# Attention and gated FFN on one core: other orders of work for its 32 rounds, and two moved steps

## The chip, the cores and the metric

The kernel runs on one core of one Trainium2 chip. The metric is device microseconds of that core for one execution; lower is better. The core's engines are named as the profile names them: PE (TensorE, with PEld for its weight loads), DVE (VectorE), ACT (ScalarE), POOL (GpSimd) and SP (SyncE, which here only issues DMAs). Each engine works through its own queue in order, and engines wait for each other by semaphores.

## What is computed

Input x has 2048 rows of 448. Two branches are mixed row by row with a gate g:

```python
qkv = (x @ wqkv).reshape(B, S, 3, H, Dh)                 # H = 16 heads, Dh = 28
p = softmax(einsum("bhqd,bhkd->bhqk", q, k) * Dh ** -0.5)
a = einsum("bhqk,bhkd->bhqd", p, v) @ wo
gate = x @ W_gate; gate = gate * (gate > 0)              # F = 1792
b = (gate * (x @ W_up)) @ W_down
g = sigmoid((x * gate_w).sum(-1))
out = g * a + (1 - g) * b
```

All inputs and the output are float32. For accuracy, most operands are split into a high part and the rest ("low"), and a product is a sum of several matmuls: 11 of them (TERMS) for a product over 448, three for the down projection.

## The kernel before

**Stages.** A prologue (up to about 96 us) casts x and the projection weights, computes queries and keys of the first heads and all values, and begins with head 0. Then come 32 **rounds**, two for each head: round v handles half of the keys (8 tiles of 128) of head v // 2 for all 2048 queries. A tail finishes the gate-and-up products, does the down projection and the output projection `wo`, mixes and stores.

**Orders written out by hand.** What is issued in a round stands in a string (R0 to R31, lines 49 to 91; the list ROUNDS, line 93, says which round uses which). The loop from line 787 reads the letters one by one. Each letter issues one step, and since every engine's queue is in order, the string sets the order on all of them:

- x: one of the 11 matmuls of a unit of the query-and-key projection (`qk_mm`) or of gate and up (`gu_mm`), 128x128 by 512 columns. After the eleventh, the result leaves PSUM: a gate unit by ACT (`relu`), an up unit by DVE (`hidden`), then DMAs.
- s: `score`, two matmuls for 2 x 512 scores. Part of the scores (raw) are copied to SBUF by ACT, and DVE also reads them from PSUM, in b; the others (direct), whose row maximum is already in the query's extra rows, go through ACT's exp at once.
- m: `smax`, two matmuls of scores of a later head of which only the maximum is kept (DVE). n: `smax_end`, which transposes those maxima and sends them by DMA into that head's queries.
- b: `block_min`, running minimum of negated raw scores (DVE). A: `all_max`, which makes of it the maximum for each query (DVE, several small steps). g: `take_max`, subtraction of that maximum from a tile of 2048 (POOL). e and E: `take_exp`, exp of half or all of such a tile (ACT).
- P and Q: `pv`, the two halves of the product of exps and values, with PE as four independent column groups of 32. c and f: `rescale`. N: `normalise`, on POOL, of the head before, which needs a DMA of reciprocal row sums. w: casts of gate-and-up weights. D: casts of down weights.

**PSUM.** s and m take turns over three buffers of two banks each (`ps_w`, line 137), so each of them can only start once the one three before has been read out. x units, P and n share two further banks (`ps_x`).

**Around the two moved steps.** In the prologue, `qk(tb, c)` is one unit: block tb of 512 rows, output rows c. Unit 0 of all four blocks holds keys and queries of head 0; its results go to DRAM by POOL's DMA queue, in turns through one of two forms (line 463), and `load_k(0)` and `load_q(0)` (lines 542, 543) read them back on SP's and POOL's queues. In the tail a list `todo` (lines 968 to 980) is run in order. `down(i)` is 12 matmuls with h tile i; `gate_up(i)` is 22 matmuls, followed by the load of weights for tile i + 2 into the freed one of two buffers, and by the write of h. Four of the 56 gate-and-up tiles, 52 to 55, are left for the tail (`done` = 52): 52 and 53 ahead of the first `down`, 54 and 55 between later ones.

Of the kernel before, what the change touches and what calls it, by code (L numbers as in the profile page):

```python
# [48 lines left out]
R0 = "xxbbsssxxxxsxbxmxxxsxxxxxssxxxxsxAxsxxxxxxmxxxxxgsbsxexxebxxsxxxgmxbxxmePAeQ"

R1 = "nsmsxxsgbxbxsxxxgxsxxbxsxxxsxsxxxssAxxmxxsxmsxxmxxxmxgmgExexxxxsxmsxsxxexbsxxbEcxxebmxPeNAfQ"

R2 = "smsxggbxxsxsxxxsxxbxsbxxxxxssxxxsxxAxggsmxxsxsxExxxmmsxxxmxxxsxsxexbxxxxbxsmebxeeAexPemmQ"

R3 = "gsmNsxsbxsxwxsbbExxxAxxssmxxwxgxxsxxxxxxxwxmEmcsnxxxgxgxxsxxxsxmxsxxxxmmxfExsxxmxxxssbbsbeePAQw"

R4 = "smsxxsbxxxwwxxsxxbsgbxxxsxxmsxsxxsxsxsAxmxwxsxxsmsgxgxxxExxbxmxxeexmmxxgxsPbxEesxembwQAx"

R5 = "NsxxsxxssbgxxxbxxxxwbxxxxsmnxsxsmAsxxswgsxsxxEmxxmxxxxsxxsxmxxEmxxmgsbxexxxxsxxmbegxscbefPeAwwQ"

R6 = "smsxxxxgxbwssgxxxxxxxsxxxbbxxwemxAssxxxssxsxxmxxsxxsmsxgxexmmsexgbexxxxxsEbemPsewmxwQbxAx"

R7 = "wssxxbxxsNbxxsbxxxxxgwxsxxxsxmsxsxxxxAsxsgxsxxmnxmxxxesxwsgexmmxxsxbsxxxxcexxsbbAexxmPEgmexfemQw"

R8 = "smsxgxxswsxxxbxsxwbxbxxsxAxsxxssxgxsmxxgsxxsxmgxxExmxsEmxxmxxwxsxmsbPExxexbmxsxbAxexwQx"

R9 = "ssxsxbxsxxbxbxxxNxxsxsxAxgxggssxxxxsxsxmmExxsxxmxxsxxmwxmxsxxwmxwexsxnesEbbcsPxgmbxeAxxxxfxemQw"

R10 = "sxswxxsgxxxxxbsxwxsxgbwbxsxxAxxesxgxxxxssxxmsxxsxxmsxexmxsxEmxxmxxsxgxbwmEmPEmsxbsxxQbA"
# [12 lines left out]

R17 = "smsxxbxsxxsxbNxbxxsxgxsxxxssxxAxxnxssmxxexxxmxsmxgxxmesxxsxmgxxEmExgmsxxcxxbxsexbsfbePAQ"

R18 = "xgsmsxbxsxxxbxxsbxxsxxAsxxxsgsxxssxxxxmsxexmxxxsxxgsmxxemxexxmxesmgEePsebmxxsbbxAQ"

R29 = "sxxsxxssxxxbxxxxgxxEbgxxsxxbxxsxsxsxxNxxxxsAxxsxssnxsxxxcxsxxxxxxggExxExxsbxxxxexbxxsbeAfPQxx"

R30 = "DsxxsxgxsxxxxxsxbxsbxxExxxbxxxxssxAxxxxgxsgxsxxsxxxsssxxxxxxxsxEsxxgxExxbexxxxxsebDxxxPbQxA"

R31 = "xxsxxsbxxxxxxsxxbxssxbxxxxxsxxsxxxsxsxxsxxxAxxgxEgxxxxexxxxxgxgsexxNDxexxexxxexDexcsfxPQ"
# [20 lines left out]
def gated_mix_kernel(ctx, tc, x, wq, wo, wgu, wd, out):  # L112
# [40 lines left out]
    def low(dst, src, high):  # L153
        nc.vector.tensor_tensor(dst, src, f32(high), op=OP.subtract)  # L154
# [148 lines left out]
    def all_max():  # L303
        v, j, quads = todo_all.pop(0)
        to = ((0, 11) if j == 2 else (9, 10))[v % 2]
        a, b = (1 - v % 2, 9) if j == 2 else (1, 9 + v % 2)
        nc.vector.tensor_reduce(MN[:, 1:3], R2.pop((v, j)).rearrange("p a (b r) -> p a b r", r=32), axis=AX.X, op=OP.min,  # L307
                                apply_transpose=True)
# [68 lines left out]
    with tc.tile_pool(name="qkv", bufs=1) as pa:
        W = pa.tile([P, 7, VO + VC], F32R, name="W")

        def load_w(c):  # L380
# [82 lines left out]
        def qk(tb, c, terms=TERMS, among=()):  # L463
            ps = ps_any(f"qk_{tb}_{c}")
            for n, (a, b) in enumerate(terms):
                nc.tensor.matmul(ps, W[:, a, c * P:(c + 1) * P], xf(tb, b), start=(n == 0), stop=(n == NT - 1))
# [9 lines left out]
            nc.gpsimd.dma_start(qk_d[c * P:(c + 1) * P, :, tb * TB:(tb + 1) * TB], f32(st))
# [558 lines left out]
```

## Time and profile before

| | |
|---|---|
| median of 3 runs | 1195.46 us (1195.09 to 1198.18) |
| the profiled execution, its own time | 1196.28 us |
| its span from first to last instruction | 1194.5 us |
| PE / PEld busy | 1183.0 / 821.9 us |
| DVE / ACT / POOL busy | 896.9 / 879.0 / 743.3 us |
| mean granted PE clock | 0.999 |

A matmul's shown duration is longer than the distance between two matmuls in a stream, because they are pipelined. So a short wait between two matmuls is not seen as idle time of PE. It is seen in the spacing of their starts, in the length of a stretch that holds a known number of matmuls, and in what PEld, the weight load in front of a matmul, waited for.

In the rows of waits, the numbers are the total in us, how many times, and the longest. In rows of a stretch (A:B), they are its length, then the busy time of PE, PEld, DVE, ACT and POOL with the count of instructions, then the granted PE clock, the share of DMA and GB/s. In rows of the timeline they are the start and the duration in us, the engine, the line, the operation and what it writes and reads; in brackets the idle time before it and what ended it. In rows of groups they are busy us and the mean in ns, then the idle time before them.

### The profile page before, as it was taken

Reading aid. Unit: us, or ns where it says so; the run is one execution under the profiler, and the core shown is the slowest. Engines: PE = TensorE matmul, PEld = TensorE weight load, DVE = VectorE, ACT = ScalarE, POOL = GpSimd, SP = SyncE. Lnnn points to the kernel's source line nnn. Section 1 sums busy time; section 2 is a strip of 40 time slices with the busy share of each in tenths; the row PEclk is TensorE's granted clock in tenths of the full one; section 3 lists DMA queues with packets and bytes.
Section 4 is the critical chain, followed back from the end, with each engine's and each line's share of the span. In section 5 each row is a group of like instructions: output and inputs, shape, how many; then the busy total and the mean of one; then the engine's idle time right before and its main releaser. Section 6 shows DMA issues by size and latency. Waiting matters only on the chain. (4 is left out here: it accounts for less than half of the span.)

```text
span 1194.5 us, 16947 instructions
## 1 busy us (share of the span) xinstructions
PE 1183.0 (99%) x6183; PEld 821.9 (69%) x6183; DVE 896.9 (75%) x1173; ACT 879.0 (74%) x1018; POOL 743.3 (62%) x325
## 2 busy tenths in 40 slices
PE   9999999999999999999999999999999999999998
PEld 6886666666666666666666566666666666899997
DVE  5577888898988888998888898989888553443342
ACT  5237889899999888888888888888888984322121
POOL 5323677898989786777776676767686773421020
PEclk9999999999999999999999999999999999999999
DMA  9994564636373644343445525153534336643342
GB/s 307 283 398 142 193 215 153 179 123 209 120 203 113 211 145 147 116 127 83 142 130 192 144 95 159 41 159 106 155 130 162 121 122 207 210 144 110 116 135 79
DMA packets 70667, 188.86 MB, mean 158 GB/s; under 512 B 13958, under 2 KB 20558, under 8 KB 65678
## 3 DMA queue, kind: packets, MB, share of 16 engines
q1 hardware_dynamic: 65624, 167.31, 45.0%
q0 software_dynamic: 4480, 19.99, 4.4%
q8 instruction: 49, 0.80, 0.3%
q10 hardware_dynamic: 480, 0.47, 0.1%
q14 instruction: 34, 0.28, 0.1%
HBM read 126.96 MB, written 60.96 MB: 157 GB/s over the span
## 5 line engine op out<-in xcount | busy, mean ns | idle before, releaser
L321 POOL TENSOR_TENSOR P<-P,rm 128x2048 f32<-128x2048 f32 x102 | 470.5, 4633 | 118.6 <-DVE rm L315 85.1
L645 PE MATMUL gu<-X,wg 128*128 128x512 f32 x1232 | 365.8, 398 | 2.1 <-DMA wg<-ws_d 2.1
L240 DVE TENSOR_REDUCE mx<-sm 128x1 f32<-128x1024 f32 x256 | 304.3, 1216 | 57.0 <-PE sm L236 55.1
L342 PE MATMUL s<-Q,K 128*128 128x512 f32 x1024 | 319.6, 402 | 2.6 <-DVE mx L240 0.9
L645 PEld LDWEIGHTS gu<-X,wg 128*128 128x128 f32 x1232 | 231.7, 189 | 73.5 <-issue 13.4
L342 PEld LDWEIGHTS s<-Q,K 128*128 128x128 f32 x1024 | 181.9, 188 | 82.5 <-DVE r L292 15.8
L348 ACT ACTIVATE P<-s 128x1024 f32<-128x1024 f32 x204 | 202.0, 1028 | 39.6 <-PE s L342 37.7
L704 PE MATMUL po<-P,V 128*32 128x512 f32 x1640 | 229.9, 595 | 0.0
L346 ACT ACTIVATE P<-s 128x1024 f32<-128x1024 f32 x206 | 201.8, 1032 | 15.8 <-PE s L342 14.0
L332 ACT ACTIVATE P<-P 128x1024 f32<-128x1024 f32 (+1 forms) x154 | 202.1, 1344 | 1.4 <-POOL P L321 1.1
L292 DVE SCALAR_TENSOR_TENSOR r<-s,r 128x1024 f32<-128x1024 f32 x124 | 151.8, 1224 | 20.8 <-ACT P L348 10.2
L236 PE MATMUL sm<-K,Q 128*128 128x512 f32 x520 | 160.7, 398 | 1.4 <-DMA Q<-qk_d 1.4
L704 PEld LDWEIGHTS po<-P,V 128*32 128x32 f32 x1640 | 60.9, 109 | 110.6 <-issue 107.5
L704 PE MATMUL po<-V 128*32 128x512 f32 x408 | 136.8, 594 | 0.0
L321 POOL TENSOR_TENSOR V<-V,rm 128x2048 f32<-128x2048 f32 x24 | 111.2, 4633 | 23.3 <-ACT P L348 18.0
L236 PEld LDWEIGHTS sm<-K,Q 128*128 128x128 f32 x520 | 93.3, 188 | 33.8 <-ACT P L346 4.5
L148 ACT ACTIVATE hh<-hr 128x512 fp32r<-128x512 f32 x52 | 32.8, 632 | 109.2 <-PE acc L939 109.2
L154 DVE TENSOR_TENSOR hh<-hr,hh 128x512 fp32r<-128x512 f32 x52 | 46.6, 900 | 74.1 <-ACT hh L148 73.8
L939 PE MATMUL acc<-WD,hh 128*128 128x448 f32 x480 | 99.3, 365 | 0.0
L939 PEld LDWEIGHTS acc<-WD,hh 128*128 128x128 f32 x480 | 90.1, 188 | 7.3
L292 DVE SCALAR_TENSOR_TENSOR r<-s,P 128x1024 f32<-128x1024 f32 x50 | 61.1, 1223 | 23.7 <-ACT P L348 23.6
L307 DVE TRANSPOSE_TENSOR_REDUCE mn<-r 128x32 f32<-128x1024 f32 x63 | 77.9, 1237 | 1.2
(93 smaller groups left out, 1134.7 us busy)
## 6 DMA issues: line engine op xcount, KB each, us to landing
wg<-ws_d SPq DMA_DIRECT2D x42, 896.0 KB
K<-qk_d SPq DMA_DIRECT2D x32, 448.0 KB
X<-x_d SPq DMA_DIRECT2D x56, 256.0 KB
h_d<-h SPq DMA_DIRECT2D x56, 256.0 KB
Q<-qk_d SPq DMA_DIRECT2D x62, 224.0 KB
hr<-h_d SPq DMA_DIRECT2D x52, 256.0 KB
ws_d<-wg SPq DMA_DIRECT2D x14, 896.0 KB
x_d<-X POOLq DMA_DIRECT2D x8, 1024.0 KB, 15.0
```

Source lines behind the costliest of these rows:

```text
L236: nc.tensor.matmul(ps[:, c, :], Q[h][:, u * P:(u + 1) * P], K[h % 3][:, k0:k0 + TB], start=True, stop=True)
L240: nc.vector.tensor_reduce(to, ps, axis=AX.XY, op=OP.max)
L292: nc.vector.scalar_tensor_tensor(r, ps, -1.0, before, op0=OP.mult, op1=OP.min)
L307: nc.vector.tensor_reduce(MN[:, 1:3], R2.pop((v, j)).rearrange("p a (b r) -> p a b r", r=32), axis=AX.X, op=OP.min, apply_transpose=True)
L321: nc.gpsimd.tensor_tensor(QUAD[q], QUAD[q], m, op=OP.subtract)
L332: nc.scalar.activation(q, q, AF.Exp, scale=-SCALE)
L342: nc.tensor.matmul(ps[:, c], K[h % 3][:, k * P:(k + 1) * P], Q[h][:, j * TB:(j + 1) * TB], start=True, stop=True)
L346: nc.scalar.activation(dst, ps, AF.Exp, scale=SCALE)
L348: nc.scalar.activation(dst, ps, AF.Copy, scale=-1.0)
L645: nc.tensor.matmul(ps, WS[i][:, s, a], xf(i // NF, b), start=(n == 0), stop=(n == NT - 1))
L704: nc.tensor.matmul(po[32 * j:32 * j + 32], V[:, h // 4 % 2, k, h % 4], AT.pop((v, k, j)), start=(k == k0), stop=(k == k0 + NK // 2 - 1))
L939: nc.tensor.matmul(ACC[i // NF][t][:, :D], HH[i][:, a, t * P:(t + 1) * P], wd_high_low(f, b), start=(f == 0 and n == 0), stop=(f == NF - 1 ...
```

## The change

Three edits. (1) All orders are replaced by others with the same counts of s, m, b, g, A per round and, over all rounds, the same 1320 x; rounds 11 to 28 use two orders in turns, R11 and R12, where before they used eight. (2) In the prologue, unit 0 of block 3 is issued before unit 2 of block 1 instead of after it. (3) In the tail, `gate_up(54)` follows `down(4)` instead of `down(2)`, and `gate_up(55)` follows `down(6)` instead of `down(4)`. The diff, with the orders cut to those that the text speaks of most (R0 to R10 and R29 to R31 are replaced in the same way; R13 to R18 fall away):

```diff
-R11 = "sxsxbsxxbgxxxsxxxxsbxxxgsxxsxxssAxsmgnsxxmsxmNxsmxmEExxxxmmsxxxxbxscxxseexxbgefebxxxmAPQ"
-R12 = "sxgssbxgxxxxsbxxxsbxxxxsxxsxssxxsAxmxxsxxsmEmxxsxmxxgxxExmxsgxbsbxsPbExxeAxemmmQ"
-R13 = "sxxsxgxbssxbexbNxxxgxxxsxxxsxxsxxxAsxxsxmnxcsxxsmexxxgxgsmsexxmxxmsxsbxbxxsexEbxeAPmfmemQ"
-R14 = "xsmsxxsbxxxgsexxxxbbAsxxxxsxxsssxxsxxmxgxxgxxsmxsxemxxmsExmxxxxssmPgEbebmsbAxexQx"
+R11 = "ssbnsxxxxsxbxNxbxxggsxxxxsxxxsxsxxssxxAmxsxxemsxmxexxmsxmxxemmgexsbxxxsbcxxxsbxAxmgeePefeQ"
+R12 = "gsmsxxxxssebxxbbxxxsxxxxmxAexxssxgxsxxsxxsmxxsxxemsmexgxexmxxxmsxmxexsbxsgebsebAPQ"
...
 ROUNDS = [
     R0, R1, R2, R3, R4, R5, R6, R7,
-    R8, R9, R10, R11, R12, R13, R14, R15,
-    R16, R17, R18, R11, R12, R13, R14, R15,
-    R16, R17, R18, R11, R12, R29, R30, R31,
+    R8, R9, R10, R11, R12, R11, R12, R11,
+    R12, R11, R12, R11, R12, R11, R12, R11,
+    R12, R11, R12, R11, R12, R29, R30, R31,
 ]
...
         qk(2, 1)
+        qk(3, 0)
         qk(1, 2)
-        qk(3, 0)
         split_w(*w4)
...
-        if i % 2 == 0 and 0 < i and done + 1 + i // 2 < NB * NF:
-            todo.append((gate_up, done + 1 + i // 2))
+        if i % 2 == 0 and 2 < i and done + i // 2 < NB * NF:
+            todo.append((gate_up, done + i // 2))
```

More of the change, by code (lines that the diff above doesn't have):

```diff
@@ L47 @@
 NP = 10
[L49 to L69, printed above, removed]
@@ L71 @@
-R11 = "sxsxbsxxbgxxxsxxxxsbxxxgsxxsxxssAxsmgnsxxmsxmNxsmxmEExxxxmmsxxxxbxscxxseexxbgefebxxxmAPQ"
-R12 = "sxgssbxgxxxxsbxxxsbxxxxsxxsxssxxsAxmxxsxxsmEmxxsxmxxgxxExmxsgxbsbxsPbExxeAxemmmQ"
-R13 = "sxxsxgxbssxbexbNxxxgxxxsxxxsxxsxxxAsxxsxmnxcsxxsmexxxgxgsmsexxmxxmsxsbxbxxsexEbxeAPmfmemQ"
-R14 = "xsmsxxsbxxxgsexxxxbbAsxxxxsxxsssxxsxxmxgxxgxxsmxsxemxxmsExmxxxxssmPgEbebmsbAxexQx"
-R15 = "sNmsxxsxsxxxbgxbxsbxxnxsxxsxsxsxAxxxsmsExgxmxxmxscxsxexmxxxmgxmxxmxxxEsxxbxsxsbePgefebAQ"
-R16 = "sxmsxgxsxxsxxbexbxsxxgxbmAxxxsxsgsxxxxssxmxxsxxsxemxmxgsExxmxxxssmEebPbsmexQxbAxx"
@@ L83 @@
[L83 to L91, printed above, removed]
+R11 = "ssbnsxxxxsxbxNxbxxggsxxxxsxxxsxsxxssxxAmxsxxemsxmxexxmxsmxxemmgexsbxxxsbcxxxsbxAxmgeePefeQ"
@@ new lines @@
+R12 = "gsmsxxxxssebxxbbxxxsxxxxmxAexxssxgsxxsxxsxxmxxsxxemsmexgxexmxxxmsxmxexsbxsgebsebAPQ"
+R0 = "bsxxsbxxxxbsxxssAxxxxxxsxxsxxxmsxxgsxxxxmxsxxsxbgxxxxxxxxbEsxxemxbxxxmxeAPQ"
+R1 = "nsgmsxxssNxxxxxbgxxEbbsmxxxxxxssxsxxxxAsxmxsxxxsExxxmxgmsxxxmxxxxxExmsxmgxxxxxscbssbebAPefQ"
+R2 = "smsxbxxssxbxxxsgxxxsbxgxxxsmsxAxsxsxsxsmxxxxxsxmxEgxxxmmsxxbxxxsexsexgexxxxxbmexxebAxmePQ"
+R3 = "nsgmsxxsgswxxbxwxxbbeAxxssxxxxxsxsxxsexmxxwxmxsNxxxsxmExmxxmxsgxxxxsxxxgmemsxxxxexsxbcbxsPebAfeQw"
+R4 = "smsxxxssbxxxxswxgbwxxbxsxxgsxsAxxsswxxmxgsxexmsxxxsxxmxexsmgxxsxbxxxxxxExxbsExembxemwPQAm"
@@ new lines @@
+R5 = "gsxsxxsbgsxbxxxxxwwxxxbxsmxxwxwsxssAxxxxsmxsxxxnssmxgxExmxmsxxNxxEmxxxmssgEbePbcmsbfeAxxxxxQ"
+R6 = "wssbsxxxxgbsxbxxgxxxxxwxssxxxmwxsmxxsAxsxxxsxxsmxexsxeemxxxgxmsgxxemxxxmxeesseePsbwxbmQbxAx"
+R7 = "ssxNxbwxgssxxxbbxxxxxAxwxswxsxxxsxxxssxmxxxxwEgxmmxnxsxsxxmsxEmxxgxmsxemxxxmgsxbsexbsecbfeAPQ"
+R8 = "wxsmsbxgxxsxxswxxgxbxsbexxxsxxxssxxxAxgssxxxmxxsxmsxxxmexsxxmemegxwsxbEPmsxxbxemxsexbxAwxQ"
+R9 = "sxwsNxxggswsxxxxxxxxxbsxbbxsxxsxsAxxsxxsxgemmxgxsxsxxxmxemxsxmxnEwxxwxxxmsmbEPemscxxsebfbxxAQ"
@@ L93 @@
+R10 = "wsxxxgssxxgxsbxxxxbxwxxxsbxwxsxxsxxsxsAsgxsxxxxmxxxemsxmxexxxmsxExxmxsmbgxxsPEebemmsbAwQ"
+R29 = "sxxsxsxxxbxgxsxxbsxExsxxxxxxxxxbxssxsxAxxxsxgNxxsxsxxxssxxxxgxsxxxExxxbxgxxbxExsexxcxexfxPbAQn"
+R30 = "sgsxxsbxxsxxxxxbxxgxEbxxxxxsxxxxxsssxxxxxsxxsxAsxxxxexgxxxxsxsExxxsexxxbgxxxxsexbxxsexDDbxPQA"
+R31 = "sxsxxsxxxbxxxxxsbbxxxxxxxgsxxxxsxxssxxxxAsxxsxxgxgxgExxxDxxxxNxxxExxEsexcexxsxxfxxxDxPQ"
 ROUNDS = [
     R0, R1, R2, R3, R4, R5, R6, R7,
-    R8, R9, R10, R11, R12, R13, R14, R15,
-    R16, R17, R18, R11, R12, R13, R14, R15,
```

## The prediction

> **What bounds the kernel now.** I read the page first, then who waits on TensorE (PE) and on its weight loads (PEld), then the stretches of the rounds, and the timeline at the three places that the change touches.
>
> ```profile
> span 1194.5 us, 16947 instructions
> PE 1183.0 (99%) x6183; PEld 821.9 (69%) x6183; DVE 896.9 (75%) x1173; ACT 879.0 (74%) x1018; POOL 743.3 (62%) x325
> ```
> ```profile
> PE gu L645 <- DMA wg<-ws_d: 2.1, 1, 2.1
> PE sm L236 <- DMA Q<-qk_d: 1.4, 1, 1.4
> ...
> PEld s L342 <- DVE r L292: 15.8, 39, 0.8
> ...
> PEld s L342 <- ACT P L346: 5.2, 22, 0.5
> ```
>
> PE is busy 1183.0 of 1194.5 us, so only time that PE loses can be won. Two open waits stand out: 2.1 us for gate-and-up weights, 1.4 us for the first query. The rest hides inside "busy", because a matmul's shown duration (about 0.4 us) is longer than its spacing: the weight loads in front of score matmuls wait for VectorE (DVE) or ScalarE (ACT) to empty a PSUM buffer. How much PE loses by that I take from the stretches of the rounds (first number the length; a round ends where its last PV matmul does):
>
> ```profile
> 96.16:410.61 314.45, 313.18 (x1688) 199.86 (x1686) 270.67 (x355) 280.16 (x325) 246.17 (x105) 1.00 0.54 172
> 410.61:914.04 503.43, 502.98 (x2722) 318.21 (x2719) 443.90 (x585) 436.65 (x456) 360.25 (x109) 1.00 0.43 132
> ...
> 150.93:180.12 29.19, 29.19 (x161) 18.77 (x157) 25.90 (x35) 24.84 (x27) 20.95 (x5) 1.00 0.68 218
> 467.33:522.85 55.52, 55.52 (x307) 35.50 (x303) 50.14 (x65) 48.74 (x52) 39.37 (x13) 1.00 0.45 132
> 410.61:467.33 56.72, 56.57 (x306) 34.99 (x302) 49.50 (x69) 48.40 (x50) 41.51 (x13) 1.00 0.50 152
> 941.50:968.71 27.21, 27.21 (x152) 17.98 (x150) 15.14 (x24) 24.41 (x26) 19.87 (x6) 1.00 0.32 98
> ```
> ```profile
> 1025.60 5.32 PE L645 MATMUL gu<-X,wg 128*128 128x512 f32 x22
> 1030.75 0.57 PE L939 MATMUL acc<-WD,hh 128*128 128x448 f32 x2
> ```
>
> The last window row is round 30, my yardstick: its order holds 54 x and 16 s, so 54 + 2·16 = 86 full matmuls, and P beside Q, in 27.21 us, with no wait of PE listed. One matmul more is (1030.75 − 1025.60)/22 = 0.234 us. Orders R11 and R12 hold 40 + 37 x, 32 s and 16 m: 77 + 64 + 32 = 173 matmuls = 2·86 + 1, so a clean pair is 54.65 us. Rounds 11 to 28 hold nine such pairs, 491.8 us clean, and took 503.43: **11.6 us lost**. Rounds 0 to 10 hold 465 x, 172 s and 84 m, 977 matmuls, clean 11·27.21 + 31·0.234 = 306.6, and took 314.45: **7.9 us lost**.
>
> **The change, part by part.**
>
> *1. P beside Q.* Where full matmuls stand between P and Q, PE leaves and enters the four-column form of PV once more. Round 12 has x and m there:
>
> ```profile
> 460.51 0.60 PE L704 MATMUL po<-P,V 128*32 128x512 f32 x3
> ...
> 460.94 0.60 PE L704 MATMUL po<-P,V 128*32 128x512 f32 x3
> ...
> 461.48 0.96 PE L645 MATMUL gu<-X,wg 128*128 128x512 f32 x3
> 462.28 1.55 PE L236 MATMUL sm<-K,Q 128*128 128x512 f32 x6
> 463.76 3.64 PE L704 MATMUL po<-P,V 128*32 128x512 f32 x32
> ```
>
> Leaving takes 461.48 − 460.94 = 0.54 us where the step inside PV is 0.43. Entering takes 463.76 − (462.28 + 5·0.234) = 0.31 instead of 0.234. Parted costs 0.54 + 0.31 − 0.43 − 0.23 = 0.19 us; starts of single matmuls overlap by some 10 ns, so I take 0.2. In the old orders 18 rounds part P from Q (2, 4, 6 to 10, and 11 of rounds 11 to 28), in the new ones five (5, 6, 8, 9, 10): 13·0.2 = **2.6 us less**, 2.2 of it in rounds 11 to 28.
>
> *2. Waits for PSUM.* Scores and maxima (s, m) share three two-bank buffers in turn, so each waits until the one three before it is emptied. Old R11 shows the price of a short distance:
>
> ```profile
> 419.53 0.63 PE L342 MATMUL s<-Q,K 128*128 128x512 f32 x2
> ...
> 420.17 0.30 PEld L236 LDWEIGHTS sm<-K,Q 128*128 128x128 f32 x2 [0.45 <-ACT P L346]
> ```
> ```profile
> L240 DVE TENSOR_REDUCE mx<-sm 128x1 f32<-128x1024 f32 x256 | 304.3, 1216 | 57.0 <-PE sm L236 55.1
> ```
>
> This m follows s, s, x and s; its buffer is that of the first s, whose last matmul ends 0.17 us (0.4 less a step) after its step, so up to the m there are 5·0.234 − 0.17 = 1.0 us of PE work, about as long as one eviction by ACT and shorter than one by DVE (1.216). I counted this distance for all 729 uses in both sets of orders: under 1.1 us, 8 before and none after; under 1.3 us, 63 before and 26 after; in rounds 11 to 28, 45 before and 18 after. So waits should shrink, but a distance isn't a time, since the emptying engine may have other work first. Bounds: all waits gone (each round as clean as round 30), or each pair as bad as the worst old pair, R11 with R12, at 56.72. I take the rows of old R13 with R14 as nearest: 55.52 − 54.65 − 2·0.2 for two parted PVs leaves 0.47 us of waits per pair, with five distances under 1.3 us; the new pair has two. Rounds 11 to 28 then come to 9·(54.65 + 0.47) = 496.1: **7.3 us less**, 2.2 of them from part 1. In rounds 0 to 10, 7.9 − 7·0.2 = 6.5 us are waits; these orders also carry weight casts, and round 2, a plain one of 92 matmuls, lost 29.19 − 27.21 − 6·0.234 = 0.58, of it 0.2 parted. I take 0.4 a round, 4.4 in all: 2.1, and 0.4 from part 1, **2.5 us less**. The three last rounds hold one x more each, the early ones three fewer: nothing in sum.
>
> Other letters move with the orders. n, the transpose of a head's maxima, is the fourth letter of new R11 (the 38th before), so its two small DMAs enter SP's queue some 8 us of PE work sooner, when all maxima of that head are in. N, a product on POOL that needs a DMA, stands in front of that round's first subtractions, as it did in old R13 and R15, which saw no such wait. I cost both at nothing; a late DMA under N would move the subtractions of that round, rival D's mechanism.
>
> *3. Halves of exps.* The new R11 and R12 take every exp in halves (e), where the old orders of rounds 11 to 28 had 35 whole ones (E):
>
> ```profile
> L332 ACT ACTIVATE P<-P 128x1024 f32<-128x1024 f32 x104 | 108.4, 1066 | 1.4 <-POOL P L321 1.1
> ...
> L332 ACT ACTIVATE P<-P 128x2048 f32<-128x2048 f32 x50 | 95.4, 1920 | 0.0
> ```
>
> 35·(2·1066 − 1920) ns = 7.4 us more ACT work. With it ACT has 436.65 + 7.4 = 444 of 496 us, and DVE its 443.9: both 90%. PE covers it; without that cover it is 7.4 us, or 0.4 a round.
>
> *4. The tail.* After down 2 PE stood still for weights of gate-and-up tile 54:
>
> ```profile
> 1004.33 7.46 PE L939 MATMUL acc<-K,hh 128*128 128x448 f32 x36
> 1004.90 0.37 SPq L630 DMA_DIRECT2D wg<-ws_d  x1
> ...
> 1013.09 0.69 DVE L154 TENSOR_TENSOR hh<-hr,hh 128x512 fp32r<-128x512 f32 x1
> ...
> 1013.94 6.96 PE L645 MATMUL gu<-X,wg 128*128 128x512 f32 x22 [2.15 <-DMA wg<-ws_d]
> 1014.59 0.33 SPq L630 DMA_DIRECT2D wg<-ws_d  x1
> ```
> ```profile
> 1014.00:1016.00 2.00, 2.00 (x5) 1.61 (x6) 0.00 (x0) 0.00 (x0) 0.56 (x1) 0.50 0.62 178
> 1018.00:1020.00 2.00, 2.00 (x10) 1.63 (x9) 0.00 (x0) 0.00 (x0) 0.00 (x0) 1.00 0.97 359
> ```
>
> Now downs 3 and 4, 24 matmuls at 7.46/36 = 0.207, fill 1011.8 to 1016.7, and the weights are there at 1013.9. Down 4 needs its cast, done at 1013.78; it starts at 1014.2. Won: the 2.15 us. Behind the wait the granted clock was 0.50, and the 22 matmuls took 6.96 where the next 22 took 5.32: another 1.6, and 0.1 for the first weight load. **3.9 us less**. Tile 55's weights, issued at 1014.59, take the same 9 us, 1023.6, and are wanted at 1016.7 + 5.15 + 4.9 = 26.8: no new wait. The moved step's own write of h and ACT's relu go with it; ACT no longer stands before that relu, so casts and the loads behind them on SP's queue come sooner.
>
> The Trainium skill's page "TensorE: Matmul & The Clock Gate", section "What's actually happening", says that the clock halves after an idle window of about 3.4 us. By it a gap of 2.15 us is too short to count and the tail would give 2.25 us. The row of 0.50 says otherwise here.
>
> *5. The prologue.* Head 0's queries and keys wait for unit 0 of all four blocks; that of block 3 now runs one unit (11·0.234 = 2.6 us) sooner.
>
> ```profile
> 21.96 2.40 DVE L154 TENSOR_TENSOR X<-xr,X 128x1024 fp32r<-128x1024 f32 x2
> ...
> 32.17 0.67 POOL L476 DMA_DIRECT2D qk_d<-K  x1 [1.35 <-DVE K L154]
> ...
> 35.56 1.03 POOL L211 DMA_DIRECT2D Q<-qk_d  x2 [2.71 <-DMA qk_d<-K]
> 36.24 2.05 SPq L211 DMA_DIRECT2D Q<-qk_d  x2
> ...
> 47.14 0.70 PE L236 MATMUL sm<-K,Q 128*128 128x512 f32 x2 [1.39 <-DMA Q<-qk_d]
> ```
>
> Block 3 is cast by 24.4, and its unit would start near 25.3: nothing to wait for. But sends alternate, so it now leaves in two DMAs by the other buffers, and the other unit's write stands before the query loads on POOL's queue. Of 2.6 us some 1.5 remains at the loads. They land among other transfers, so bounds are 0 and 1.5 (the 1.39 and the first load's delay); I take **1.2 us less**.
>
> *Sum:* 7.3 + 2.5 + 3.9 + 1.2 = 14.9 us off the profiled execution's 1196.28 (its span and 1.8 around it): 1181.4. The runs' median is 0.8 below that execution, so **1180.6 us**.
>
> **Rivals.**
>
> *A, the waits only move.* Three buffers and engines at 90% may shift each wait to the next use. Then parts 1, 4 and 5 remain: 1196.28 − 2.6 − 3.9 − 1.2 − 0.8 = 1187.8. For it: most uses between 1.3 and 2 us keep a similar count, 264 before and 325 after. Against: single waits above 0.1 us stand at the short distances.
>
> *B, all rounds clean.* 11.6 + 7.9 − 5·0.2 + 5.1 = 23.6 less: 1171.9. Round 30 does it, but without maxima.
>
> *C, nothing to measure.* The two new orders are repeated nine times, a bad wait with them: nine pairs like old R11 with R12, less its parting, 56.5 us, are 508.6, 5.2 over before. With 2.5 + 3.9 + 1.2 won elsewhere, 1193. The change would then not do what its words say ("more distance"). Against: 18 short uses instead of 45.
>
> *D, slower: exps too late for Q in odd rounds.* New R11 ends "AxmgeePefeQ": P beside Q, with the last two exps behind P.
>
> ```profile
> 417.33 1.25 DVE L307 TRANSPOSE_TENSOR_REDUCE mn<-r 128x32 f32<-128x1024 f32 x1
> ...
> 419.97 0.71 DVE L315 STREAM_TRANSPOSE rm<-mn 128x512 f32<-128x512 f32 x1
> ```
> ```profile
> L321 POOL TENSOR_TENSOR P<-P,rm 128x2048 f32<-128x2048 f32 x102 | 470.5, 4633 | 118.6 <-DVE rm L315 85.1
> ```
>
> Its second all_max stands 9.6 us into the round's PE work; it takes 420.68 − 417.33 = 3.35, two subtractions 9.27, an exp 1.07: 23.3, where Q starts at 24.0. Late by more than 0.7 us, Q waits. Three DVE evictions more in front, 3.7 us, would cost 3.0 in each of nine odd rounds, 27 us. With parts 1, 4 and 5 and no other wait won: 1187.8 + 27 = 1215. Against: DVE may run that step ahead of its place, as its inputs are complete after the block minima 6 us earlier.
>
> **How the numbers follow.** Chances: forecast (1176 to 1185) 0.48, A 0.23, B 0.13, C 0.10, D 0.06. The range 1171.5 to 1191 leaves out C, D and what of B lies lower. No change means within 0.3%, 3.6 us. Forecast, A and B lie below that, 0.84 and a little of C: faster 0.85, same 0.09, slower 0.06.
>
> **What would show it.** Right: rounds 11 to 28 near 496 us, pairs near 55.1; the weight loads' waits for DVE before scores well under 15.8 us; no wait of PE for weights and no clock of 0.50 past 1000 us; the wait for the first query under 0.4. Wrong: a pair above 55.9, PV matmuls spaced over 0.43 in odd rounds, ACT without idle time, or a new wait of PE in the tail.

## The result and the profile after

| | before | after |
|---|---|---|
| median of 4 runs each | 1195.53 us (1195.09 to 1198.18) | 1184.28 us (1184.05 to 1184.62) |
| the profiled execution, its own time | 1196.28 us | 1184.21 us |
| its span | 1194.5 us | 1182.4 us |

The ratio after to before is 0.9901, with a 95% interval of 0.9884 to 0.9919. The forecast was 1180.6 us with a range of 1171.5 to 1191: the sign and the range hold, and the time is 3.7 us above the forecast.

The first lines of the page of after, the span and the busy time of each engine:

```profile
span 1182.4 us, 17006 instructions
PE 1175.0 (99%) x6183; PEld 821.2 (69%) x6183; DVE 894.1 (76%) x1173; ACT 877.2 (74%) x1054; POOL 743.3 (63%) x325
```

ACT has 36 instructions more (1054 against 1018): the exps that are now taken in halves. PE has the same 6183 matmuls in a span 12.1 us shorter.

Who waits, in the trace of after (total us, times, longest):

```profile
PEld s L330 <- DVE r L280: 10.4, 36, 0.8
PEld s L330 <- DVE mn L289: 9.2, 11, 0.8
PEld s L330 <- ACT P L334: 5.4, 24, 0.7
PEld sm L224 <- ACT P L334: 4.6, 22, 0.4
...
PE s L330 <- DVE mx L228: 0.9, 1, 0.9
PE s L330 <- DVE mn L590: 0.4, 1, 0.4
PE s L330 <- ACT P L334: 0.2, 1, 0.2
```

The line numbers are 12 lower than before, so L330 is the old L342. The two open waits that the prediction named (2.1 us for tile 54's weights, 1.4 us for the first query) are no longer in the list. The weight loads' wait for DVE's r is 10.4 us where it was 15.8. The 9.2 us under DVE's mn (1.7 before) are hardly waits for a buffer: these 11 waits are 0.84 us each and stand at the first score of a round, right behind PV, where before the same 0.84 stood under other names (mx, rm, r). So this list alone doesn't measure what the rounds won; the lengths of the stretches do.

The stretches of after (length, busy PE, PEld, DVE, ACT, POOL with counts, clock, DMA share, GB/s), and then two pairs of the new orders R11 and R12, rounds 13 and 14, and 15 and 16:

```profile
0.00:95.67 95.67, 92.70 (x401) 74.11 (x401) 61.84 (x71) 39.36 (x80) 35.17 (x59) 1.00 0.89 313
95.67:406.81 311.14, 310.72 (x1683) 200.89 (x1684) 269.20 (x353) 279.84 (x327) 245.32 (x104) 1.00 0.54 169
406.81:905.06 498.25, 498.11 (x2723) 317.29 (x2719) 442.02 (x585) 435.05 (x491) 359.68 (x110) 1.00 0.45 136
905.06:985.76 80.70, 80.67 (x451) 53.10 (x447) 41.96 (x65) 71.62 (x76) 64.24 (x23) 1.00 0.38 114
985.76:1182.40 196.64, 192.81 (x940) 175.86 (x936) 79.11 (x101) 51.34 (x81) 38.90 (x31) 1.00 0.48 149
462.37:517.59 55.22, 55.22 (x306) 35.30 (x303) 48.81 (x64) 48.09 (x54) 39.91 (x12) 1.00 0.44 129
517.59:572.90 55.31, 55.31 (x306) 35.32 (x302) 49.03 (x66) 48.53 (x55) 39.83 (x12) 1.00 0.37 108
```

Before, the same five stretches were 96.16, 314.45, 503.43, 79.88 and 200.58 us. So the span of 12.1 us less is 0.5 before the rounds, 3.3 in rounds 0 to 10, 5.2 in rounds 11 to 28 and 3.9 in the tail, less 0.8 that the last three rounds take more. The pairs lie near 55.3: nine in 498.25 are 55.36 each, against 55.94 before and the 54.65 of a clean pair.

The tail of after, at the place where PE stood still before (timeline: start, duration, engine, line, operation):

```profile
994.78 1.37 SPq L618 DMA_DIRECT2D wg<-ws_d  x1
...
1005.90 2.60 PE L927 MATMUL acc<-WD,hh 128*128 128x448 f32 x12
...
1008.34 3.91 PE L633 MATMUL gu<-X,wg 128*128 128x512 f32 x16
```
```profile
1008.00:1010.00 2.00, 2.00 (x11) 1.64 (x10) 0.00 (x0) 0.00 (x0) 1.94 (x2) 1.00 0.95 360
```

Tile 54's weights are issued at 994.78, 9.0 us after the last PV matmul (985.76). Two downs more fill the time until they are there, tile 54 starts without idle time ahead of it, and its matmuls run at clock 1.00, where the row of before had 0.50.

### The profile page after: what moved, and what is told of

It reads as the page before. It is cut to its first block, busy times and chain, and to the rows that moved or that the text cites. A ratio compares the mean times of both kernels' runs of the same rounds, so it can differ in the third digit from the quotient of the medians.

```text
span 1182.4 us, 17006 instructions
## 1 busy us (share of the span) xinstructions
PE 1175.0 (99%) x6183; PEld 821.2 (69%) x6183; DVE 894.1 (76%) x1173; ACT 877.2 (74%) x1054; POOL 743.3 (63%) x325
## 4 chain that ended last, share of the span: by engine, by line
PE 96%; DVE 1%; DMA 1%; ACT 1%; issue 0%; SPq 0%; DVEq 0%; ACTq 0%
PE gu L633 24%; PE s L330 20%; PE po L692 19%; PE acc L927 12%; PE sm L224 10%; PE v L469 3%; PE wo L886 3%; PE qk L641 3%; PE qk L454 2%; DVE r L280 1%; DMA wr<-wq 0%; DMA X<-x_d 0%; ACT P L336 0%; ACT V L336 0%; SPq L414 0%
## 5 line engine op out<-in xcount | busy, mean ns | idle before, releaser
L633 PE MATMUL gu<-X,wg 128*128 128x512 f32 x1232 | 358.9, 395 | 0.1
L330 PE MATMUL s<-Q,K 128*128 128x512 f32 x1024 | 315.9, 403 | 1.7 <-DVE mx L228 0.9
L330 PEld LDWEIGHTS s<-Q,K 128*128 128x128 f32 x1024 | 180.7, 188 | 82.4 <-DVE r L280 10.4
L692 PE MATMUL po<-P,V 128*32 128x512 f32 x1640 | 227.4, 594 | 0.0
L320 ACT ACTIVATE P<-P 128x1024 f32<-128x1024 f32 (+1 forms) x182 | 208.5, 1171 | 0.5 <-POOL P L309 0.2
L224 PE MATMUL sm<-K,Q 128*128 128x512 f32 x520 | 163.2, 400 | 0.1
L224 PEld LDWEIGHTS sm<-K,Q 128*128 128x128 f32 x520 | 91.9, 188 | 34.1 <-ACT P L334 4.6
```

The lines of the kernel that those rows point to most:

```text
L224: nc.tensor.matmul(ps[:, c, :], Q[h][:, u * P:(u + 1) * P], K[h % 3][:, k0:k0 + TB], start=True, stop=True)
L320: nc.scalar.activation(q, q, AF.Exp, scale=-SCALE)
L330: nc.tensor.matmul(ps[:, c], K[h % 3][:, k * P:(k + 1) * P], Q[h][:, j * TB:(j + 1) * TB], start=True, stop=True)
L633: nc.tensor.matmul(ps, WS[i][:, s, a], xf(i // NF, b), start=(n == 0), stop=(n == NT - 1))
L692: nc.tensor.matmul(po[32 * j:32 * j + 32], V[:, h // 4 % 2, k, h % 4], AT.pop((v, k, j)), start=(k == k0), stop=(k == k0 + NK // 2 - 1))
```

## The experiments

Times are medians; each ratio is to runs of the kernel before on the same chip. The stages of every profile, in us, each read from its stretches:

| kernel | median | ratio, 95% interval | before round 0 | 0–10 | 11–28 | 29–31 | tail |
|---|---|---|---|---|---|---|---|
| before | 1195.53 | | 96.16 | 314.45 | 503.43 | 79.88 | 200.58 |
| after | 1184.28 | 0.9901 (0.9884 to 0.9919) | 95.67 | 311.14 | 498.25 | 80.70 | 196.64 |
| e1 tail alone | 1193.03 | 0.9979 (0.9966 to 0.9991) | 96.20 | 314.70 | 503.35 | 79.90 | 197.05 |
| e2 query unit alone | 1194.66 | 0.9990 (0.9974 to 1.0007) | 95.23 | 314.43 | 503.41 | 79.91 | 199.52 |
| e3 orders alone | 1186.09 | 0.9928 (0.9913 to 0.9943) | 96.64 | 311.19 | 498.67 | 80.74 | 196.66 |
| e11 after, old tail | 1185.54 | 0.9918 (0.9904 to 0.9931) | 96.39 | 311.09 | 499.04 | 80.75 | 197.13 |
| e4b old R13, R14 | 1216.54 | 1.0171 (1.0151 to 1.0190) | 96.42 | 311.08 | 528.37 | 80.68 | 197.65 |
| e4 the same, joined | 1250.06 | 1.0452 (1.0425 to 1.0479) | 96.51 | 311.10 | 565.69 | 80.71 | 197.39 |
| e5 before, joined | 1239.56 | 1.0366 (1.0349 to 1.0383) | 95.93 | 328.07 | 537.33 | 79.88 | 201.09 |
| e6 after, parted | 1195.36 | 1.0009 (1.0000 to 1.0019) | 95.47 | 311.03 | 508.81 | 80.73 | 196.56 |
| e8 late all_max | 1234.67 | 1.0336 (1.0320 to 1.0351) | 96.11 | 311.15 | 547.87 | 80.74 | 196.63 |
| e9 short distances | 1189.06 | 0.9950 (0.9938 to 0.9963) | 96.60 | 311.00 | 502.24 | 80.71 | 196.65 |
| e10 longer distances | 1187.06 | 0.9934 (0.9922 to 0.9947) | 97.12 | 311.09 | 500.86 | 80.73 | 196.60 |
| e7 short maxima | 1183.33 | 0.9900 (0.9886 to 0.9914) | 94.54 | 311.52 | 496.79 | 80.74 | 196.61 |

**The three edits, each by itself.** e1 is the kernel before with the tail's edit alone:

```diff
-        if i % 2 == 0 and 0 < i and done + 1 + i // 2 < NB * NF:
-            todo.append((gate_up, done + 1 + i // 2))
+        if i % 2 == 0 and 2 < i and done + i // 2 < NB * NF:
+            todo.append((gate_up, done + i // 2))
```

> The kernel before with the tail edit alone: gate-and-up tiles 54 and 55 two downs later. Theory (the open wait and the halved clock behind it are both part of the price): 3.9 us less than before, 1191.6; no wait of PE for wg in the tail, no stretch with a granted clock of 0.50 after 1000 us, 22 gate-and-up matmuls in 5.2 to 5.3 us. Rival (only the open wait is won, the clock falls anyway): 2.2 us less, 1193.3, with a stretch of 0.50 left.

Its tail is 197.05 us, 3.5 less than before, with no wait for weights and the clock at 1.00 throughout: the edit does what the prediction said. That rests on the profiles. By medians it is worth 2.5 us, with an interval of 1.1 to 4.1, which holds the 3.9 of the theory and the 2.2 of the rival.

e2 is the kernel before with the query unit's edit alone:

```diff
         qk(2, 1)
+        qk(3, 0)
         qk(1, 2)
-        qk(3, 0)
```

> The kernel before with the prologue edit alone. Theory (the first query comes 1.1 us sooner, but the prologue's end is paced by DVE's maxima, so part is given back before round 0): first sm at 46.0 instead of 47.1, round 0 begins 0.4 to 0.7 us sooner, time 0.3 to 0.7 less than before, 1195.0. Rival (the prediction's term holds in full): round 0 begins 1.1 or more sooner, 1194.3.

The ratio's interval contains 1. The first m starts at 46.18 us in place of 47.14, and round 0 begins 0.9 us sooner, between the 0.4 to 0.7 of the theory and the 1.1 of the rival. Two rows of its timeline show what is left of that wait, and the wait in its (old) tail, here 1.40 us:

```profile
46.18 0.70 PE L236 MATMUL sm<-K,Q 128*128 128x512 f32 x2 [0.33 <-DMA Q<-qk_d]
...
1012.24 2.13 PE L645 MATMUL gu<-X,wg 128*128 128x512 f32 x8 [1.40 <-DMA wg<-ws_d]
```
```profile
1012.20:1017.20 5.00, 4.96 (x21) 4.05 (x22) 0.55 (x1) 0.00 (x0) 1.28 (x1) 1.00 0.96 280
```

After a wait of 1.40 us the clock stays at 1.00. After the 2.15 us of the kernel before it was 0.50.

e3 is the kernel before with all new orders, and with the old query unit and tail. e11 is the kernel after with the old two lines in the tail (the reverse of e1's diff).

> The kernel before with all new orders, but the prologue and the tail as they were. Theory (the three edits add up): the rounds give 7.7 us (from round 0 to the end of round 31 890.1 us instead of 897.8), 1187.8; the wait for wg and the halved clock in the tail stay. Rival (the edits need each other): the rounds take over 892 us.

> The changed kernel with the old lines for the last block's gate and up tiles: orders and query unit as changed, the tail as before. Prediction's view (the tail's edit is worth 3.9 us by itself: 2.15 us of wait for the weights of tile 54 and 1.6 us at half clock): 3.9 us longer, near 1188, with that wait and a stretch at 0.50 past 1000 us. Theory from the run with the new orders alone (the last rounds' new orders already bring the tail's first loads and casts sooner, so the old tail has no wait there): within 0.6 us of the changed kernel, 1183.7 to 1184.9, no wait for weights and no stretch at 0.50.

e3's rounds last 311.19 + 498.67 + 80.74 = 890.6 us, as in after (890.1). The surprise is its tail: 196.66 us, the length of after, though the tail's code is the old one. In e11 the old tail costs 0.5 us more than the new one, with this wait ahead of tile 54 and the full clock behind it:

```profile
1005.44 5.42 PE L633 MATMUL gu<-X,wg 128*128 128x512 f32 x22 [0.30 <-DMA wg<-ws_d]
```
```profile
1006.00:1008.00 2.00, 2.00 (x10) 1.61 (x9) 0.00 (x0) 0.00 (x0) 1.07 (x1) 1.00 0.99 249
```

So the 3.9 us of the tail have two sufficient causes. With the old orders the tail's edit brings 3.5; with the new orders it brings 0.5 or less, because these alone already bring tile 54's weights in time. The timeline of e3 has the issue of these weights and the start of the tile's matmuls, without idle time:

```profile
996.04 0.38 SPq L618 DMA_DIRECT2D wg<-ws_d  x1
...
1004.94 5.30 PE L633 MATMUL gu<-X,wg 128*128 128x512 f32 x22
```

The issue comes 996.04 − 987.24 = 8.8 us after the last PV matmul; before it was 1004.90 − 993.92 = 11.0. Those 2.2 us are as long as the wait that is gone. Most of them are there already at the DMA of row sums ahead of it on SP's queue, which is issued 1.1 us after the last PV matmul in e3 (988.31) and 2.7 us after it in the kernel before (996.65). What makes that one sooner was not followed further.

**The two orders that the prediction took as nearest rows.** e4b puts old R13 and R14 in place of R11 and R12 in rounds 11 to 28 of the kernel after; e4 does the same with P moved to stand right ahead of Q.

```diff
-R11 = "ssbnsxxxxsxbxNxbxxggsxxxxsxxxsxsxxssxxAmxsxxemsxmxexxmxsmxxemmgexsbxxxsbcxxxsbxAxmgeePefeQ"
+R11 = "sxxsxgxbssxbexbNxxxgxxxsxxxsxxsxxxAsxxsxmnxcsxxsmexxxgxgsmsexxmxxmsxsbxbxxsexEbxeAPmfmemQ"
-R12 = "gsmsxxxxssebxxbbxxxsxxxxmxAexxssxgsxxsxxsxxmxxsxxemsmexgxexmxxxmsxmxexsbxsgebsebAPQ"
+R12 = "xsmsxxsbxxxgsexxxxbbAsxxxxsxxsssxxsxxmxgxxgxxsmxsxemxxmsExmxxxxssmPgEbebmsbAxexQx"
```

> The same with old R13 and R14 as they stood, P and Q parted. If their rows of before carry over, rounds 11 to 28 take 9 x 55.52 = 499.7, 1.4 more than in the changed kernel: 1185.7. The difference to the run with P beside Q is the price of 18 partings: 3.6 us by the prediction's 0.2 each, 5.4 by 0.3.

> The changed kernel with the old orders R13 and R14, P moved to stand right before Q, in place of the new R11 and R12 in rounds 11 to 28. By the prediction's price of 0.2 us for each parting these rounds take 9 x (55.52 - 0.4) = 496.1 us, 2.2 less than the 498.25 of the changed kernel: 1182.1. Rival (a parting costs 0.3, as the second matmul behind each exit from PV also comes 0.1 late): 494.3, 1180.3. Rival (moving P back makes a new wait): no less than with P where it stood.

Both expectations fail, by 31 and 68 us. In e4b these orders, which cost 55.52 us a pair in their old place, cost 528.37/9 = 58.7 (57.80 in rounds 13 and 14, which have no stretch at half clock and no open wait for X; the first pair has both). In the old sequence R13 stood behind R12; here it stands behind R14, whose all_max ends later. POOL's subtraction at this place in the kernel before, whose round 13 begins at 467.33:

```profile
465.65 4.61 POOL L321 TENSOR_TENSOR P<-P,rm 128x2048 f32<-128x2048 f32 x1 [6.75 <-DVE rm L315]
```

The timeline of e4b, round 13, which begins near 469.5:

```profile
471.04 4.64 POOL L309 TENSOR_TENSOR P<-P,rm 128x2048 f32<-128x2048 f32 x1 [9.81 <-DVE rm L303]
...
475.71 1.06 ACT L320 ACTIVATE P<-P 128x1024 f32<-128x1024 f32 x1 [1.59 <-POOL P L309]
...
476.68 3.75 ACT L334 ACTIVATE P<-s 128x1024 f32<-128x1024 f32 x4
...
477.74 0.30 PEld L330 LDWEIGHTS s<-Q,K 128*128 128x128 f32 x2 [0.50 <-ACT P L334]
```

POOL's subtraction starts 1.5 us behind the round's begin where it was 1.7 us ahead of it, the exp at the head of ACT's queue waits for it, the copies of scores out of PSUM queue behind that exp, and PE waits for the copies. An order's waits are not its own: they belong to it and to the order ahead of it.

**P beside Q.** e5 is the kernel before with P moved right ahead of Q in all 18 rounds that part them (and, in seven other orders, past letters that issue nothing on PE), for example:

```diff
-R14 = "xsmsxxsbxxxgsexxxxbbAsxxxxsxxsssxxsxxmxgxxgxxsmxsxemxxmsExmxxxxssmPgEbebmsbAxexQx"
+R14 = "xsmsxxsbxxxgsexxxxbbAsxxxxsxxsssxxsxxmxgxxgxxsmxsxemxxmsExmxxxxssmgEbebmsbAxexPQx"
```

> The kernel before with P moved to stand right before Q in all 18 rounds that part them, and nothing else. Theory of the prediction (a parting costs PE 0.2 to 0.3 us each and nothing hangs on it): 3.6 to 5.4 us less, 1190 to 1191.6. Rival, formed from the runs with old R13 and R14 (a joined P and Q is 6.9 us in which PE gives ACT and DVE nothing new; the old orders have no exps and minima queued there, so the engines fall behind and PE waits for PSUM after it): slower than before by 5 us or more.

It is 3.7% slower. What stood behind P now stands ahead of it, so PE reaches it 3.44 us sooner (half a PV, 8 steps of 0.43), before the engines have emptied the buffers that it needs, and PE waits in the open. Waits of e5:

```profile
PE sm L236 <- DVE r L292: 23.7, 22, 2.5
PE s L342 <- DVE r L292: 6.0, 5, 2.5
PE gu L645 <- DMA wg<-ws_d: 2.3, 1, 2.3
```

Part of the loss is the clock: seven stretches of 3.41 us at clock 0.50 stand in the rounds, behind such waits. Round 12, without such a stretch, takes 30.3 us from the last PV of the round ahead to its own last PV; rounds 20 and 28, the same order with one, take 31.7 and 31.95. By that some 10 of the 47 us that the rounds take more are half clock (an estimate).

e6 goes the other way in the kernel after: in R11 and R12 one x out of a run of four is put between P and Q.

```diff
-R11 = "ssbnsxxxxsxbxNxbxxggsxxxxsxxxs...xsbxAxmgeePefeQ"
+R11 = "ssbnsxxxxsxbxNxbxxggsxxxsxxxs...xsbxAxmgeePxefeQ"
-R12 = "gsmsxxxxssebxxbbxxxsxxxxmxA...sebAPQ"
+R12 = "gsmsxxxxssebxxbbxxxsxxxmxA...sebAPxQ"
```

> The changed kernel with one x taken from a run of four x and put between P and Q, in R11 and in R12: 18 partings more, and what ACT and DVE have queued is the same. By the prediction's price of 0.2 us each 3.6 us slower, 1187.9; by 0.3 (the second matmul behind the exit from PV is late too) 5.4 slower, 1189.7. Rival (a parting costs nothing, as the time at the exit is a drain that other work covers): within 1 us of the changed kernel.

Rounds 11 to 28 take 508.81 us, 10.6 more and twice the highest size expected: 0.59 a parting. The direct part can be read from the timeline of e6:

```profile
487.88 0.59 PE L692 MATMUL po<-P,V 128*32 128x512 f32 x1
488.40 0.50 PE L633 MATMUL gu<-X,wg 128*128 128x512 f32 x1
488.83 0.63 PE L692 MATMUL po<-P,V 128*32 128x512 f32 x3
```

From the last step of P to the first of Q are 488.83 − 487.88 = 0.95 us; a PV step of 0.43 and an x of 0.234 would be 0.66. So leaving and entering cost 0.29 here, not 0.2. Some of the rest of the 0.59 is what the x is missed for at the place that it left: in round 13 the weight load of the score behind the shortened run waits 0.34 us, where in after it has no such wait. That this is all of the rest is not shown.

**Distance.** e9 takes away distance in after: two x in R11 and one in R12 are moved behind a use that they stood ahead of (1.45 and 1.22 us of PE work become 0.98). e10 gives distance at the two places where the trace of after shows single waits.

```diff
 e9
-R11 = "...xxAmxsxxemsxmxexxmxsm..."
+R11 = "...xxAmxsxemsmxxxexxmxsm..."
-R12 = "...mxxsxxemsmexgx..."
+R12 = "...mxxsxemsmxexgx..."
 e10
-R11 = "...emsxmxexxmxsmxx..."
+R11 = "...emsxxmxexmxsmxx..."
-R12 = "gsmsxxxxssebxxbbxxxsxx..."
+R12 = "gsmsxxxssebxxbbxxxxsxx..."
```

> The changed kernel with R11 and R12 altered in one thing: in R11 two x, in R12 one x are moved behind a maximum or score that followed them, so that in each order one short use of the three buffers comes back (distance 0.98 us of PE work in place of 1.45 and 1.22). Nothing else moves; P stays beside Q. Theory of the prediction (the distance between a use and the third before it decides whether PE waits): about 0.28 us at the place in R11 and 0.1 to 0.4 us in R12, in nine rounds each, so 5 to 7 us longer than the changed kernel, rounds 11 to 28 at 503 to 505 us in place of 498.25, near 1190. Rival (what frees the buffers is late for other reasons, the queues of VectorE and ScalarE, and distances of about 1 us are no worse than of 1.3): under 1.5 us of difference, 1184 to 1186.

> The changed kernel with the two places given more distance at which its trace shows single waits: in R11 one x is moved ahead of the maximum that waits 0.11 us in some rounds (distance up 0.23, the next maximum keeps its own), in R12 one x is moved ahead of the score that waits 2 times 0.076 us in some rounds. Theory (distance decides): 1 to 2 us less over the eighteen rounds, 1182 to 1183.5. Rival (the waits move to the next use, as the engines that empty the buffers have queues of their own): within 0.7 us of the changed kernel, 1183.6 to 1185.

e9 takes 502.24 us in rounds 11 to 28, 4.0 more, of which 0.4 is a wait for X that has nothing to do with it: some 0.2 us a round, of the right kind but three quarters of the lowest size expected. The waits of e9 name what the shorter distances meet, with the count of such waits up from 22 to 34:

```profile
PEld sm L224 <- ACT P L334: 10.4, 34, 0.7
```

The place in its trace, round 13, on ACT and on the weight loads:

```profile
475.28 0.63 ACT L649 ACTIVATE rl<-gu 128x512 f32<-128x512 f32 x1
475.75 1.08 ACT L334 ACTIVATE P<-s 128x1024 f32<-128x1024 f32 x1
```
```profile
476.88 0.30 PEld L224 LDWEIGHTS sm<-K,Q 128*128 128x128 f32 x2 [0.65 <-ACT P L334]
```

The m needs the buffer of a score whose copy ends at 475.75 + 1.08 = 476.83. The copy is late by the 0.63 us of a relu that ACT ran just before it. R11 and R12 hold seven x units in two rounds, so such a relu falls on this place in rounds 13, 17, 21 and 25 only, and there PE loses 0.38 us more than elsewhere. Without the relu the shorter distances cost less, but not nothing: the m ahead of this place comes 0.11 and 0.10 us late in all of these odd rounds, and an m of R12 0.08 and 0.10.

e10 gains nothing: 500.86 us, of which 1.9 are waits for X (below), so 499.0 against 498.25. The wait at the m of R11 goes, and the score two uses later gets one of 0.12; the wait at the score of R12 goes, and the next score gets one of 0.09. At these distances the waits only move.

**DVE's share in what is left.** e7 shortens DVE's eviction of a maximum by taking it over 64 of the 512 keys of a bank.

```diff
-        nc.vector.tensor_reduce(to, ps, axis=AX.XY, op=OP.max)
+        nc.vector.tensor_reduce(to, ps[:, :, :64], axis=AX.XY, op=OP.max)
```

> The changed kernel, but each block maximum of the scores is taken over 64 of the 512 keys of each bank, an eighth of them; what the softmax subtracts is therefore another shift. Each eviction of a maximum by VectorE is about 1 us shorter, so VectorE, 90% busy, is relieved by some 1 us at each of 256 maxima. Theory (what is left of waits in rounds 11 to 28, 0.71 us a pair, hangs on VectorE's evictions): rounds 11 to 28 come to 492 to 495 us in place of 498.25, rounds 0 to 10 lose 2 to 4 us as well, so 1176 to 1181. Rival (the rest is the exit from and entry into PV, and ScalarE's queue): under 1.5 us less, 1183 to 1184.5.

The group of these reductions and the stretch of rounds 11 to 28 in e7:

```profile
L228 DVE TENSOR_REDUCE mx<-sm 128x1 f32<-128x128 f32 x256 | 73.8, 288 | 180.5 <-PE sm L224 180.2
```
```profile
406.06:902.85 496.79, 496.79 (x2722) 319.81 (x2718) 316.29 (x585) 434.98 (x491) 359.90 (x110) 1.00 0.45 136
```

DVE falls from 442.0 to 316.3 busy us in these rounds, and PE wins 1.5 us, 0.8 of it in the first and the last pair, which in after hold small waits for X. The rival holds: with the distances of the new orders, the evictions of maxima by DVE set almost none of what is left.

**Rival D, brought about.** e8 puts the first all_max of R11 behind three maxima.

```diff
-R11 = "...sxsxxssxxAmxsxxemsxmxexxmx..."
+R11 = "...sxsxxssxxmxsxxemsxmAxexxmx..."
```

> The changed kernel with the first all_max of R11 moved behind three m on DVE. Rival D of the prediction (exps come too late for Q): all_max runs about 7 us later, as it had run ahead of its place, its two subtractions and exps with it; PE waits 3 us or more within P or Q in each of nine odd rounds, 27 us or more, over 1211. Rival (the margin covers it): under 3 us slower.

Rounds 11 to 28 take 49.6 us more, 5.5 in each odd round. Timeline of e8, round 13, on DVE, and then on PE:

```profile
483.23 1.23 DVE L295 TRANSPOSE_TENSOR_REDUCE mn<-r 128x32 f32<-128x1024 f32 x1
...
485.83 0.71 DVE L303 STREAM_TRANSPOSE rm<-mn 128x512 f32<-128x512 f32 x1
486.46 4.58 DVE L228 TENSOR_REDUCE mx<-sm 128x1 f32<-128x1024 f32 x4
```
```profile
487.71 1.19 PE L224 MATMUL sm<-K,Q 128*128 128x512 f32 x4 [2.86 <-DVE mx L228]
...
494.56 0.73 PE L224 MATMUL sm<-K,Q 128*128 128x512 f32 x2 [0.61 <-DVE r L280]
```

The 3.2 us of all_max now stand between two evictions of maxima on DVE, and PE waits 2.86 us for the second. A second wait follows at the last m, behind an exp that waits for POOL. In six odd rounds the first wait is followed by 3.41 us or more at clock 0.50, and there the second wait is 0.6 us or none; it is 2.2 in rounds 15, 25 and 27, where the clock stays at 1.00. All nine take 33.5 to 34.1 us, so the half clock costs nothing here: what it takes, the second wait gives back, and the late exp sets the length of the round. P and Q themselves don't wait.

## Why the prediction was right or wrong

The forecast against the profiled execution's own time was 1181.4; it was 1184.21, 2.8 over. Rounds 11 to 28 miss by 2.1 and the prologue by 0.7. The last 0.9 of the 3.7 us is the offset between that execution and the median: the runs of after lie on their profiled execution (1184.28 and 1184.21), not 0.8 below it.

**Rounds 11 to 28: right in sign, mis-sized.** Predicted 7.3 us less, measured 5.2: a pair has 0.71 us over a clean one, not 0.47. The measured 498.25 lies 2.1 above the forecast of 496.1 and 3.0 below the 501.2 that rival A would give. The step that failed is taking old R13 with R14 as nearest rows. e4b shows that those rows don't carry over to another sequence: the same two orders cost 58.7 us a pair there. The split of the 7.3 was off too. At the 0.29 that e6 shows for a parting, the eleven that go are 3.2 of the 5.2 us, which leaves 2.0 for the waits where 5.1 were forecast (an estimate: no run takes the two apart in the new sequence). The rule beside it, that the distance between a use and the third before it decides, is borne out by e9 where distances fall to 1 us (0.2 us a round), and not by e10 above that.

**What is left of a pair's 0.71** isn't settled in full. It is an average: the seven pairs of rounds 13 to 26 take 55.27 us, 0.62 over a clean one, the first and the last pair 55.56 and 55.81. With short maxima (e7) 0.09 a pair goes in the seven. In rounds 13, 17, 21 and 25 a relu on ACT ahead of a copy makes an m 0.13 + 0.11 us late. Steps of about 0.1 us at the second matmul behind a change from PV, in every round, and behind n, at one score and at the last m in every R11, stand in e7 too; what sets these was not tried.

**P beside Q: right in sign for after, too small, and wrong as a rule.** A parting costs 0.29 us at its place and 0.59 in all in e6, where 0.2 was taken. But joining P and Q in the old orders makes the kernel 3.7% slower (e5). By e5 and e6 together, a parting is a loss only where nothing needs the cover of half a PV, as in the new orders. The prediction counted the 13 partings as a gain without asking what they covered; for the new orders the question had no price, for the old ones it has one of over 40 us (some 10 of them half clock).

**Rounds 0 to 10: right in size.** Predicted 2.5 less with the x that moved to the last rounds set off; measured 3.3 − 0.8 = 2.5. No run takes its two terms, waits and partings, apart.

**Halves of exps: no cost seen, and wrong that they are 7.4 us more work.** ACT was forecast at 444 busy us in rounds 11 to 28 and has 435.05, less than before. Two halves in a row overlap, as in round 13 of after:

```profile
483.60 1.99 ACT L320 ACTIVATE V<-V 128x1024 f32<-128x1024 f32 x2
```

1.99 us for two is 0.07 over the 1.92 of a whole one, where the prediction added up two single durations.

**The tail: right in size (3.9) and in mechanism (e1), wrong in attribution.** The term was summed as if the orders left the tail as it was. e3 and e11 show that the new orders remove the same wait: with them, the tail's edit is worth 0.5 us by one pair of profiles, and nothing that medians can tell (0.9918 and 0.9901, with intervals that overlap).

**The prologue: too large.** Predicted 1.2, measured 0.5 at round 0. The first m started 1.1 us sooner; then the new R0, whose first matmuls are those of a score, waited 0.44 us for DVE:

```profile
95.67 0.74 PE L330 MATMUL s<-Q,K 128*128 128x512 f32 x2 [0.44 <-DVE mn L590]
```

And the 1.1 us is itself no firm gain. Over all the profiles here the first m starts at 46.92 to 47.20 us with the old order of units (four kernels) and at 45.89 to 47.45 with the new one (ten kernels, mean 46.65): 0.4 us less on average, and in e10 nothing, though the code ahead of that m is the same in the ten. In after the loads leave SP and POOL 2.1 to 2.6 us sooner (the first at 33.00, where it was 35.41), more than the 1.5 of the prediction. More than half of it is lost again until they have landed; to what was not found.

**The rivals.** A (waits only move) is not refuted as a whole: it put the gain of rounds 11 to 28 at the 2.2 of the partings, and the gain was 5.2, but by the price of e6 the partings are 3.2 of that. e10 shows that it holds from here on. B (all clean) and C (nothing to measure) fall. D did not occur: in after, the all_max at the first A of round 13, which begins at 462.37, ran 7.2 us into the round, ahead of its place at 9.6, as "against" had it:

```profile
469.57 1.24 DVE L295 TRANSPOSE_TENSOR_REDUCE mn<-r 128x32 f32<-128x1024 f32 x1
```

e8 shows that a late all_max is dearer than priced (5.5 us in an odd round, not 3.0), and that it hits the maxima behind it, first through DVE's queue and then through the late exp, and not Q.

## What to carry to other kernels

An order written by hand is priced only in its sequence: rows of the same order behind another one are no bound for it, and two edits that cure the same wait don't add up, so each is to be run alone and left out alone. Before joining two stretches of work on the bound engine, ask what the second one covers: here half a PV covered 3.4 us of ACT, DVE and POOL, and joining was worth 0.29 us a time where nothing needed that cover and cost over 40 us in all where something did. Where two engines near 90% empty shared buffers, distances of about 1 us between a use and the third before it cost 0.2 us a round (e9), more where the emptying engine has another instruction to run first; lengthening two of those that were left won nothing (e10), and the waits moved.

## What was not expected of the hardware

**The clock.** Behind the start-up and ahead of a kernel's last microseconds, every stretch at clock 0.50 in these profiles is 3.41 us long, or twice that. Whether a gap of PE is followed by one is not a matter of its length alone (e2's row above has 1.40 and no such stretch). In e4 PE waits nine times at the same letter of R12, each time 2.54 us long; six of these gaps were followed by a stretch of half clock and three were not. Two of the nine, and the 5 us from each of them on:

```profile
465.86 1.19 PE L224 MATMUL sm<-K,Q 128*128 128x512 f32 x2 [2.54 <-DVE r L280]
...
527.92 0.70 PE L224 MATMUL sm<-K,Q 128*128 128x512 f32 x2 [2.54 <-DVE r L280]
```
```profile
465.90:470.90 5.00, 5.00 (x26) 2.43 (x30) 4.41 (x5) 3.51 (x4) 0.00 (x0) 0.68 0.50 197
527.90:532.90 5.00, 4.98 (x38) 2.10 (x42) 4.59 (x5) 3.79 (x4) 0.00 (x0) 1.00 0.36 84
```

A mean of 0.68 over 5 us is 3.2 us at half clock: 26 matmuls were run there, and 38 in the other window. The six rounds with such a stretch take 31.2 to 31.9 us, the three without 29.8 to 30.3.

The trace's record of the clock shows what tells them apart. The nine half-clock stretches of e4 begin at 417.92, 434.99, 465.71, 588.59, 622.72, 653.44, 776.32, 899.20 and 964.05 us: all lie whole multiples of 3.413 us apart. Cut into windows on that grid, the trace has PE busy for 0.87 to 1.25 us in the window ahead of each of the six. The other three gaps lie across two windows, and the emptier window of each has PE busy for 1.58 to 1.94 us. One of each kind:

```profile
650.03:653.44 3.41, 0.87 (x5) 0.51 (x4) 2.96 (x3) 3.41 (x4) 1.13 (x1) 1.00 0.99 267
...
834.35:837.76 3.41, 1.94 (x9) 1.22 (x7) 2.53 (x3) 3.41 (x4) 2.65 (x1) 1.00 0.95 209
```

Busy time is not the whole rule: the stretches at 434.99 and 622.72 follow windows with 2.13 and 1.85 us busy, in which PE waits twice, 0.6 to 1.0 us each time. What else counts was not found.

The Trainium skill's page "TensorE: Matmul & The Clock Gate", section "What's actually happening", says that the gate looks at windows of 3413 ns that run freely, and that it halves the clock after an idle one. The length of the stretches agrees (3.41 us in the kernel before). The grid in e4, on which equal gaps are punished or not by where they lie, fits windows that run freely. That gaps of 2.15 us are punished at all doesn't fit a window that must be idle throughout. In the prediction the 1.6 us of half clock were taken as certain; by e4 they hang on where the gap falls on that grid, which may be (it was not tried) why the kernel before has runs up to 1198 us beside those at 1195.

**The first x of a new block.** In round 11 or 27 some profiles show a wait of PE for X, in kernels whose code there is that of after: none open in after, 0.3 to 1.9 us in e6, e8, e9, e10 and e11. In e10:

```profile
866.22 0.50 PE L633 MATMUL gu<-X,wg 128*128 128x512 f32 x1 [1.11 <-DMA X<-x_d]
```

What makes those loads late in one run and not in another was not found. It is as large as the differences between after and e10 or e11, so these two are not taken as slower than after at their places of change.
